# A fused attention/GLU kernel: the transposes of six token blocks in the first layer move from TensorE to the DMA queue

## Chip, cores and metric

The kernel runs on one core of one Trainium2 chip. The metric is device microseconds of one execution. The kernel before was timed three times: 381.76 us is the median, 380.99 us the lowest and 382.18 us the highest. Smaller is better. A separate execution was recorded by the hardware profiler; the durations below come from that one.

## The reference

Four layers act in turn on `x` of 2048 tokens by 448 features (bf16): attention, GLU, attention, GLU. Both attention layers use the same weights, and so do both GLU layers.

```python
x = x + A(layernorm(x), wqkv, wo)
x = x + B(layernorm(x), w_gate, w_up, w_down)
x = x + A(layernorm(x), wqkv, wo)
x = x + B(layernorm(x), w_gate, w_up, w_down)
# A: 16 heads of 28; token s attends to s, s-2, ..., s-14 (8 keys, those below 0 masked)
# B: ((x @ w_gate) * (x @ w_up)) @ w_down, inner width 1792
```

## The kernel before

**Tiling.** The tokens are 16 blocks of 128. Layer 0 takes them in five chunks: chunk 0 is blocks 0 and 1, chunk 1 blocks 2 to 5, chunk 2 blocks 6 to 9, chunk 3 blocks 10 to 13, chunk 4 blocks 14 and 15. A block is normalised on VectorE (statistics L593 and L595, the scaled block `xn_sb` L617, with the inverse deviation by ScalarE, L596 and L598). Its transpose goes to `xnTa`, where it feeds the matmuls that make K and Q (`qk_chunk`, line L356 through the helper `pair`) and V (`v_group`). `xn_sb` is a ring of five slots; a slot is free once the transpose that reads it is done.

**Two ways to transpose.** `ln_chunk` has both. If the name of layer and chunk stands in `PE_T`, TensorE transposes: for chunks 1 to 4, eight matmuls of 64x64 against an identity (L636), two running at once on the two halves of the array, into two PSUM banks, and one copy from PSUM to `xnTa` on ScalarE or VectorE (L646). Otherwise SP issues one DMA transpose of 128x512 from `xn_sb` to `xnTa` (L625). Before the change all five chunks of layer 0 are in `PE_T`; layer 2 uses the DMA for its 16 blocks, and the GLU layers use the DMA for two blocks at a time (L622). The DMA transposes of one chunk share one semaphore, and whoever needs one of the chunk's blocks waits for the chunk's full count.

**Attention.** For a group of up to 240 query tokens: `Qz` (L842, VectorE) spreads Q, scores on TensorE (L856), exponential on ScalarE (L865), mask on VectorE (L872), weighted sum on TensorE (L890), its way out of PSUM (L901, L905), normalisation (L919 to L921, L940), and the output projection (`y_blocks`). Group 0 is the first 128 tokens.

**GLU.** `b_chunk` makes gate and up (L356 with `WGU`), copies the gate out (L1014), multiplies (L1020) and projects down (L356 with `WD`).

**Order.** Nothing is scheduled at run time. Every piece of work is an "op" with a number given in the order in which it is created; `ORDER` lists for each engine the numbers in the order of issue, and `BANKS` the PSUM banks. An entry such as `372*2.4.5/363:3` puts three steps of op 363, cut into strips of 32 columns, between the matmuls of op 372 (the strips are line L359). Each engine takes its list strictly in turn: an op that waits holds up everything behind it. The two engine choices, "act" or "dve", are made by the list in which the number stands.

**The SP queue.** SP issues nearly all DMAs, in list order. The loads that matter here are numbers 72 to 83 (`WGU`, twelve pieces; a piece of the gate matrix may be issued once the one before it of the same matrix has landed, and the same for the up matrix), 84 to 87 (`wo_g`), 92 (`wo_h`), and 88 to 91 (`WD`: 88 after the last gate piece 82, 89 after the last up piece 83, 90 after 88, 91 after 89). The stores of the extra columns of `qk` to DRAM ("PW", L740) and the transposed loads of them (L751) stand in the same list.

**Numbers used below** (before / after; the change has six ops fewer, so later numbers shift by up to six):

| work | before | after |
|---|---|---|
| scaled blocks 10 to 15, VectorE | 177 180 183 186 195 198 | 177 179 181 183 191 193 |
| their transposes on TensorE | 178 181 184 187 196 199 | none |
| copy out of PSUM, or DMA transpose | 179 182 185 188 197 200 | 178 180 182 184 192 194 |
| `Qz` and scores of group 0 | 217, 218 | 211, 212 |
| first weighted sum 0, 1 | 223, 257 | 217, 251 |
| second half-V of query blocks 3 and 4 | 248 | 242 |
| first K/Q parts of chunk 3 | 456 458 460 | 450 452 454 |
| first K/Q part of chunk 4 | 534 | 528 |
| first use of `WD` | 317 | 311 |
| GLU transpose of blocks 0 and 1 | 295 | 289 |

Of the kernel before, what the change touches and what calls it, by code (L numbers as in the profile page):

```python
# [14 lines left out]
NBLK = S // 128  # L15
# [19 lines left out]
PE_T = ("00", "01", "02", "03", "04")  # L35
# [62 lines left out]
def grp_nc(g):  # L98
# [21 lines left out]
    ),  # L120
    "act": (
# [10 lines left out]
    ),  # L132
    "dve": (
# [19 lines left out]
    ),  # L153
# [7 lines left out]
    ),  # L161
}
BANKS = (
# [221 lines left out]
def build(nc, A_x, A_wqkv, A_wo, B_w_gate, B_w_up, B_w_down, out):  # L385
# [45 lines left out]
    sc = Sched()  # L431
# [731 lines left out]
```

## Time and profile before

| what | value |
|---|---|
| median of 3 runs | 381.76 us |
| the profiled execution, its own time | 381.87 us |
| its span, first to last instruction | 380.1 us |
| granted TensorE clock | 1.00 |
| DVE busy, ACT busy | 277.1 us, 194.6 us |
| DMA moved | 24.12 MB, mean 63 GB/s |

The span is what the trace shows; 1.77 us of the profiled execution's time lies around it. Busy time of TensorE is pipelined: the rows of a timeline overlap a little, so the distance from one row's start to the next one's is the time that the work takes on the engine's path. In the chain of waits (the work that ended last, followed back) the pieces do not overlap. PE stands for TensorE, DVE for VectorE, ACT for ScalarE, SPq for the DMA queue of SP.

### The profile page before, as it was taken

What the parts mean: (1) busy time and instruction counts of PE and PEld (TensorE: products, weight loads), DVE (VectorE), ACT (ScalarE), POOL (GpSimd) and SP (SyncE); (2) the same over time, 40 slices, a digit from 0 to 9 for tenths busy, and PEclk for the clock granted to TensorE, in tenths of its full rate; (3) what the DMA queues carried; (4) which work ended last, traced back from release to release, by engine and by line L of the source; (5) the groups of instructions that cost most, each with busy time, mean ns of one, the idle gap of its engine ahead of it and who ended that gap; (6) DMA issues with size and microseconds to landing.
All of it is one profiled execution on the core that took longest, in us unless ns stands there. A gap on an engine that the chain in (4) does not pass through costs nothing.

```text
span 380.1 us, 14239 instructions
## 1 busy us (share of the span) xinstructions
PE 374.5 (99%) x6388; PEld 210.7 (55%) x6388; DVE 277.1 (73%) x572; ACT 194.6 (51%) x327; POOL 5.1 (1%) x25
## 2 busy tenths in 40 slices
PE   8999999999999999999999999999999999999997
PEld 3654587544545445454866866554455454445664
DVE  7987999898795586778477989558888487274233
ACT  4999896567235565334365422546654634134110
POOL 5000000000000000000000000000000000000000
PEclk9999999999999999999999999999999999999999
DMA  8656646200522025112103125401123104104003
GB/s 259 169 149 156 148 124 104 56 18 23 97 40 45 2 50 84 33 32 56 28 2 62 28 43 111 63 10 32 25 50 71 43 3 83 26 2 98 2 2 109
DMA packets 58804, 24.12 MB, mean 63 GB/s; under 512 B 47928, under 2 KB 58616, under 8 KB 58744
## 3 DMA queue, kind: packets, MB, share of 16 engines
q1 hardware_dynamic: 58600, 23.16, 27.6%
q8 instruction: 50, 0.82, 0.9%
q14 instruction: 10, 0.08, 0.1%
q10 hardware_dynamic: 144, 0.06, 0.1%
HBM read 9.04 MB, written 3.50 MB: 33 GB/s over the span
## 4 chain that ended last, share of the span: by engine, by line
PE 95%; DVE 2%; ACT 2%; issue 0%; DVEq 0%
PE ps L356 84%; PE ps L359 4%; PE ps L856 2%; PE ps L890 2%; PE ps L510 2%; PE ps L1032 1%; ACT E_sb L865 1%; PE ps L636 0%; ACT qk L731 0%; DVE R_sb L919 0%; ACT xnTa L643 0%; DVE st L593 0%; DVE x_sb L981 0%; ACT R_sb L920 0%; ACT R_sb L921 0%
## 5 line engine op out<-in xcount | busy, mean ns | idle before, releaser
L356 PE MATMUL ps<-xnTb,WGU 64*128 64x512 bf16 (+1 forms) x1912 | 173.4, 332 | 0.1
L356 PEld LDWEIGHTS ps<-xnTb,WGU 64*128 64x128 bf16 x1912 | 93.4, 94 | 69.5 <-DVE x_sb L981 1.3
L1014 ACT ACTIVATE g_sb<-ps 128x512 bf16<-128x512 f32 x112 | 65.9, 596 | 100.6 <-PE ps L356 95.0
L1020 DVE TENSOR_TENSOR hT<-g_sb,ps 128x512 bf16<-128x512 bf16 x112 | 74.9, 682 | 55.4 <-ACT g_sb L1014 54.8
L356 PE MATMUL ps<-WD,hT 64*128 64x448 bf16 x786 | 80.6, 349 | 0.1
L356 PEld LDWEIGHTS ps<-WD,hT 64*128 64x128 bf16 x786 | 38.5, 94 | 33.0 <-issue 0.8
L356 PE MATMUL ps<-xnTa,WQK 64*128 64x512 bf16 (+1 forms) x494 | 52.3, 353 | 0.1
L981 DVE TENSOR_TENSOR x_sb<-x_sb,ps 128x448 bf16<-128x448 bf16 x62 | 36.3, 614 | 13.3 <-PE ps L356 13.2
L865 ACT ACTIVATE E_sb<-ps,shift_sb 128x1024 bf16<-128x1024 f32 (+1 forms) x36 | 37.5, 1071 | 14.1 <-PE ps L856 14.1
L593 DVE BATCH_NORM_STATS2 st<-x_sb 128x6 f32<-128x448 bf16 x64 | 38.1, 614 | 1.1 <-DMA x_sb<-in_A_x_dram 1.0
L356 PEld LDWEIGHTS ps<-xnTa,WQK 64*128 64x128 bf16 x494 | 22.8, 94 | 21.5 <-ACT E_sb L865 0.8
L731 ACT ACTIVATE qk<-ps 128x1024 bf16<-128x1024 f32 (+1 forms) x26 | 23.4, 909 | 13.9 <-PE ps L356 13.6
L617 DVE TENSOR_SCALAR xn_sb<-x_sb,mv,rstd 128x896 bf16<-128x896 bf16 (+1 forms) x64 | 28.2, 456 | 2.6 <-ACT rstd L598 2.5
L872 DVE TENSOR_TENSOR E_sb<-E_sb,MK 128x1024 bf16<-128x1024 bf16 (+1 forms) x36 | 23.4, 658 | 6.8 <-ACT E_sb L865 6.7
L356 PE MATMUL ps<-wo_g,oT 64*128 64x448 bf16 x147 | 25.5, 349 | 0.7 <-issue 0.7
L356 PE MATMUL ps<-WV,xnTa 64*128 64x336 bf16 (+3 forms) x240 | 23.1, 304 | 0.3 <-ACT xnTa L643 0.2
L920 ACT ACTIVATE R_sb<-R_sb 128x960 f32<-128x960 f32 (+1 forms) x18 | 17.2, 958 | 11.3 <-DVE R_sb L919 11.2
L919 DVE STREAM_SHUFFLE R_sb<-O_sb 128x960 f32<-128x960 f32 (+1 forms) x18 | 21.2, 1179 | 0.0
L940 DVE TENSOR_TENSOR oT<-O_sb,R_sb 128x960 bf16<-128x960 f32 (+1 forms) x16 | 17.5, 1094 | 3.9 <-ACT R_sb L921 3.9
L901 ACT ACTIVATE O_sb<-ps 128x512 f32<-128x512 f32 (+2 forms) x20 | 10.7, 558 | 16.5 <-PE ps L890 16.5
L596 ACT ACTIVATE lnv<-mv,eps_sb 128x2 f32<-128x2 f32 (+1 forms) x33 | 9.3, 290 | 16.5 <-DVE mv L595 16.3
L890 PEld LDWEIGHTS ps<-E_sb,v_sb 64*32 64x32 bf16 x1088 | 13.2, 90 | 8.0 <-issue 2.5
(68 smaller groups left out, 257.2 us busy)
## 6 DMA issues: line engine op xcount, KB each, us to landing
out_dram<-x_sb SPq DMA_DIRECT2D x15, 112.0 KB, 1.8
x_sb<-in_A_x_dram SPq DMA_DIRECT2D x3, 448.0 KB, 6.1
hT<-in_A_wqkv_dram SPq DMA_DIRECT2D x4, 224.0 KB, 4.6
WGU<-in_B_w_gate_dram SPq DMA_DIRECT2D x4, 224.0 KB, 4.1
WGU<-in_B_w_up_dram SPq DMA_DIRECT2D x4, 224.0 KB, 4.2
WD<-in_B_w_down_dram SPq DMA_DIRECT2D x2, 448.0 KB, 4.6
mv_rows<-oT SPq DMA_DIRECT2D x12, 64.0 KB, 1.8
oT<-mv_rows SPq DMA_DIRECT2D x48, 8.0 KB
```

The lines of the kernel that those rows point to most:

```text
L356: return lambda E: E.matmul(out(), lhs(), rhs(), start=start, stop=stop)
L593: sc.add("dve", one(lambda E, B=B: E.bn_stats(st6[:, B, :], x_sb[:, B, :]), ("bn", li, B)), 525.0, deps=[("x", li - 1, B)] + ([("xn", li - ...
L617: sc.add("dve", one(lambda E, B=B, dst=dst, src=src: E.tensor_scalar(dst, src, mv[:, B, 0:1], rstd[:, B:B + 1], ALU.subtract, ALU.mult), ( ...
L731: return E.activation(dst, src, ACT.Copy) if hasattr(E, "activation") else E.tensor_copy(dst, src)
L865: return E.activation(E_sb[:, slot, 2 * hp:2 * hp + 2, 0:w], ps[:, b0:b0 + 2, 0:w], ACT.Exp, bias=shift_sb[:, 0:1], scale=SCALE)
L872: return E.tensor_tensor(e, e, MK[:, kind, 0:nc].unsqueeze(1).unsqueeze(1).to_broadcast([128, 2, w // nc, nc]), ALU.min)
L890: ins.append((lambda E, b=b, c=c, o=o, vw=vw, eb=eb, eo=eo: E.matmul(ps[32 * b:32 * b + 32, bk[c], o:o + nc], vw, E_sb[64 * c:64 * c + 64, ...
L919: sc.add("dve", one(lambda E: E.stream_shuffle(R, Of, [DH] * 32), ("Rs", li, qb)), dve_est(w) + 20.0, deps=[("Oa", li, g)] + prev, prio=prio)
L940: return E.tensor_tensor(dst, O.rearrange("p d h n -> p h d n"), Rv.rearrange("p d h n -> p h d n"), ALU.mult)
L981: sc.add("dve", one(lambda E: E.tensor_tensor(x_sb[:, B, :], x_sb[:, B, :], ps[:, bk[w], 0:D], ALU.add), ("x", li, B)), dve_est(D), deps=[ ...
L1014: sc.add("act", one(lambda E, gs=gs, bk=bk: E.activation(g_sb[:, gs, :], ps[:, bk[0], :], ACT.Copy), ("G", li, j, f0)), act_est(512), deps ...
L1020: return E.tensor_tensor(hT[:, f0:f0 + nf, hs, 0:nt], v(g_sb[:, gs, :]), v(ps[:, bk[1], :]), ALU.mult)
```

## The change

Chunks 3 and 4 of layer 0 leave `PE_T`. Blocks 10 to 15 are then transposed by one DMA each (L625), six DMA transposes on SP instead of 48 matmuls on TensorE and six copies (four on VectorE, two on ScalarE). The wait list of `hT` no longer names TensorE transposes that do not exist. All lists in `ORDER` but POOL's, and all of `BANKS`, are new.

```diff
-PE_T = ("00", "01", "02", "03", "04")
+PE_T = ("00", "01", "02")
...
     "pe": (
-        "41 42 43 44 45 46 47 48 49 50 51 52 53 54 112 115 55 56 57 58 130 213 133 243 136 214 139 244 207 237 208 238 231 203 157 232 233 204 234 154 201 205 "
-        "202 206 235 160 163 236 218 327 181 328 196 252 325 223 326 187 323 184 178 324 247 257 458 248 199 459 456 460 534 461 535 457 270 329 265 530 266 "
...
+        "41 42 43 44 45 46 47 48 49 50 51 52 53 54 112 115 55 56 57 58 130 133 207 237 208 136 139 238 197 231 198 232 227 201 225 202 228 157 226 199 195 200 "
+        "196 163 229 160 154 230 212 321 246 322 319 217 320 317 241 318 251*3.5/242:2 450 452 454 453 455 451 528 323 529 264 324 259 524 260 333 525 334 456 "
...
     "dve": (
...
+        "15 17 103 39 104 16 107 108 119 117 111 120 118 114 123 125 129 126 124 132 59 131 141 135 138 61 65 137 142 62 143 40 187 144 173 171 174 172 156 185 "
+        "149 186 147 150 188 148 167 153 158 159 165 162 168 181 164 166 191 183 161 211 70 68 179 67 69 245 177 216 215 249 218 219 220 221 250 224 193 253 "
...
     "sp": (
-        "0 1 2 7 8 9 5 4 6 3 13 72 12 74 73 10 11 75 76 77 78 79 80 81 86 84 87 85 71 83 92 82 89 335 295 336 338 337 469 543 91 475 346 468 540 88 471 347 542 "
-        "90 470 398 481 480 476 401 101 102 496 99 95 98 97 94 500 96 497 100 499 498 541 93 519 548 521 523 520 522 553 547 614 617 687 685 568 689 691 569 "
...
+        "0 1 2 7 8 9 5 4 6 3 13 72 12 74 73 10 11 75 76 182 192 77 180 78 184 178 79 80 194 81 86 84 87 85 331 71 83 289 82 465 462 329 89 332 330 92 464 91 "
+        "341 463 88 340 469 90 392 475 470 395 536 98 474 97 101 102 490 534 535 100 96 93 537 493 494 492 94 491 542 99 95 513 541 514 515 516 517 608 547 546 "
...
-            war = hslot_users.get((hs, "prev"), WQKR + [("Tps", 0, B) for B in range(NBLK)] + [("vones",)])
+            war = hslot_users.get((hs, "prev"), WQKR + [("Tps", 0, B) for B in range(NBLK) if ("Tps", 0, B) in sc.ready] + [("vones",)])
```

Of the other ops each engine keeps the same ones, except that some copies out of PSUM change between ScalarE and VectorE: of the transposes that stay on TensorE, ScalarE copies blocks 7, 8 and 9 before and block 6 after, VectorE block 6 before and blocks 7, 8 and 9 after; the K/Q copy number 211 (205 after) and one of the eight copies of `WQK` (L518) go from VectorE to ScalarE. TensorE's list has 23 entries with strips before, with 70 strip steps, and 24 after, with 78.

106 rows, old and new, of tables (BANKS, ORDER) are left out of this document.

## The prediction

> **What bounds the kernel now.** I read the page's totals first, then its chain of waits.
>
> ```profile
> span 380.1 us, 14239 instructions
> PE 374.5 (99%) x6388; PEld 210.7 (55%) x6388; DVE 277.1 (73%) x572; ACT 194.6 (51%) x327; POOL 5.1 (1%) x25
> ...
> PE 95%; DVE 2%; ACT 2%; issue 0%; DVEq 0%
> ```
>
> TensorE is busy 99% of the span and holds 95% of the chain. What TensorE no longer does is saved, if nothing else makes it wait, and any new wait of TensorE is paid in full. I then looked at the stage where the six blocks are transposed: the chain from 20 to 32 us, and the group of these matmuls.
>
> ```profile
> 22.59 0.12 PE ps L636 x8
> ...
> 23.70 0.12 PE ps L636 x8
> ...
> 26.41 0.12 PE ps L636 x8
> ...
> 27.25 0.23 PE ps L636 x16
> ```
>
> ```profile
> L636 PE MATMUL ps<-hT,xn_sb 64*128 64x64 bf16 x112 | 3.7, 190 | 0.0
> ```
>
> The eight matmuls of a block hold the chain for 0.12 us. The group's 3.7 us for 112 is 0.26 us for eight, but there the head and tail of a run overlap with the next one. Next come the engines and the DMA in that stage (columns: length, PE, PEld, DVE, ACT and POOL busy, TensorE's granted clock, DMA share, GB/s):
>
> ```profile
> 20.00:30.00 10.00, 9.76 (x262) 5.07 (x256) 8.78 (x27) 9.69 (x17) 0.00 (x0) 1.00 0.56 140
> 30.00:40.00 10.00, 9.86 (x140) 4.98 (x137) 7.75 (x14) 8.51 (x11) 0.00 (x0) 1.00 0.75 181
> ```
>
> The clock is full, TensorE has under 0.3 us of idle in each ten, VectorE and ScalarE are close behind it, and the DMA engines have a quarter to a half left over.
>
> **The change, part by part.**
>
> *Removed on TensorE:* six blocks at 0.12 us are 0.72 us. Bounds: 0.72 by the chain and 6 x 0.26 = 1.6 by the group; I take 0.72, since the chain counts what TensorE's path really spends. The six copies out of PSUM (four on VectorE, two on ScalarE) cost nothing on the path while TensorE sets the pace; they give these two engines room.
>
> *Added strips:* the weighted sum of group 1 now carries two steps of the second half of V of query blocks 3 and 4.
>
> ```profile
> 28.84 0.68 PE L890 MATMUL ps<-E_sb,v_sb 64*32 64x64 bf16 x64
> 29.46 0.82 PE L356 MATMUL ps<-xnTa,WQK 64*128 64x512 bf16 x6
> 30.12 0.92 PE L356 MATMUL ps<-WV,xnTa 64*128 64x448 bf16 x8
> 30.87 0.28 PE L636 MATMUL ps<-hT,xn_sb 64*128 64x64 bf16 x8
> ```
>
> ```profile
> 72.10 0.25 PE L890 MATMUL ps<-E_sb,v_sb 64*32 64x64 bf16 x16
> ...
> 73.05 0.46 PE L356 MATMUL ps<-WV,xnTa 64*128 64x336 bf16 x4
> ```
>
> Alone such a sum takes 29.46 - 28.84 = 0.62 us. The one at 72.10 carries three steps and takes 0.95 us; a step of V is (30.87 - 30.12) / 4 = 0.19 us, so 0.95 - 0.57 = 0.38 us are its own. Two steps instead of three: I take 0.1 us saved, bounds 0 and 0.24.
>
> *Moved on VectorE: `Qz` of group 0 comes later.* Its list in the stretch before that (timeline of VectorE; the row at 18.72 is the scaled block 8, the one at 20.15 block 11, the two at 21.63 blocks 14 and 10):
>
> ```profile
> 10.47 0.64 DVE L518 COPY WQK<-hT 128x448 bf16<-128x448 bf16 x3
> ...
> 18.72 0.39 DVE L617 TENSOR_SCALAR xn_sb<-x_sb,mv,rstd 128x512 bf16<-128x512 bf16 x1
> ...
> 19.45 0.69 DVE L731 CAST qk<-ps 128x512 bf16<-128x512 f32 x1
> 20.15 0.41 DVE L617 TENSOR_SCALAR xn_sb<-x_sb,mv,rstd 128x512 bf16<-128x512 bf16 x1
> 20.48 0.61 DVE L842 TENSOR_SCALAR Qz<-qk,qmask 128x512 bf16<-128x512 bf16 x2
> ...
> 21.63 0.73 DVE L617 TENSOR_SCALAR xn_sb<-x_sb,mv,rstd 128x512 bf16<-128x512 bf16 x2
> ...
> 23.04 0.42 DVE L646 COPY xnTa<-ps 128x512 bf16<-128x512 bf16 x1
> ```
>
> ```profile
> 21.23 0.44 PE L856 MATMUL ps<-Qz,qk 64*64 64x144 bf16 x16
> ```
>
> Ahead of that `Qz` the new list has three scaled blocks of the last six (12, 14, 13) where the old one has one (11), three copies L646 (7, 9, 8) where the old one has one (6), no K/Q copy, and one weight copy less. A scaled block takes 20.48 - 20.15 = 0.33 us, a copy L646 about the same (0.42 with its overlap), the K/Q copy 0.70, the weight copy 0.2. So +0.66 + 0.66 - 0.70 - 0.2 = +0.42 us. The scores of group 0 start at 21.23, right behind `Qz`'s end at 21.09, and the ops ahead of them on TensorE are the same ones in both lists. So they come about 0.4 us later, and behind them everything on TensorE. Bounds: 0, if VectorE's waits before 18.7 us shrink, and 0.7; I take 0.4.
>
> *Moved on SP: six DMA transposes among the weight loads.* Their price is that of layer 2's (bottom two rows of this view: issue time of one on SP's queue, and time to landing):
>
> ```profile
> L625 SPq DMA_TRANSPOSE xnTa<-xn_sb x16: 1188/1200/2319, 109.3 to 243.6; - x16
> ...
> DMA to landing us min/median/max: 2.4/2.5/4.3
> ```
>
> So six of them add 7.2 us to SP's list. That queue before, where the rows at 17.99, 22.40, 30.06 and 36.31 are loads 76, 78, 81 and 82, those at 38.71 and 58.79 loads 89 and 90 of `WD`:
>
> ```profile
> 17.99 0.61 SPq L451 DMA_DIRECT2D WGU<-in_B_w_gate_dram  x1
> ...
> 22.40 0.59 SPq L451 DMA_DIRECT2D WGU<-in_B_w_gate_dram  x1
> ...
> 30.06 0.60 SPq L451 DMA_DIRECT2D WGU<-in_B_w_up_dram  x1
> ...
> 36.31 0.62 SPq L451 DMA_DIRECT2D WGU<-in_B_w_gate_dram  x1
> 38.71 0.40 SPq L451 DMA_DIRECT2D WD<-in_B_w_down_dram  x1
> ```
>
> I walk the new list from 18.6 us, the end of load 76. Block 12 is scaled at about 18.72 + 0.4 (blocks 9 and 12 instead of 8 alone) + 0.4 for its own run and overlap, say 19.6. Then: block 12 until 20.8, block 14 until 22.0, load 77 until 22.6, block 11 until 23.8, load 78 until 24.4, block 13 until 25.6, block 10 from 25.6 to 26.8. Block 10 is scaled right behind the `Qz` of group 1, at about 23.5, so SP's queue decides, not VectorE. It lands at 25.6 + 2.5 = 28.1, or at 29.9 with the longest landing of the row above; the four blocks of chunk 3 count together. Who waits: the first K/Q part of chunk 3. In the old order it starts at 29.46; without the five transposes ahead (0.6), with the V half ahead of it (0.75), the strips (-0.1) and the late scores (+0.4) it starts at about 29.9. The transposes land just in time or just late. The DMA engines were only half busy, so I take 0.2 us; bounds 0 and 2, the latter for a landing that two weight loads push back.
>
> ```profile
> DMA to landing us min/median/max: 3.4/4.2/6.3
> ```
>
> (That is the landing of the twelve `WGU` loads, whose range shows how far queueing goes: 2.1 us above the median.)
>
> The wait is felt at a second place: scaled block 15 takes the ring slot of block 10, so VectorE stops at it until chunk 3's four transposes have landed. In the new list it stands behind group 0's normalised output (L940):
>
> ```profile
> 31.41 0.68 DVE L940 TENSOR_TENSOR oT<-O_sb,R_sb 128x512 bf16<-128x512 f32 x1
> ```
>
> Fewer ops are ahead of that output now, so I put it at 29.5 to 31; behind block 15 are queued the sums and reciprocals of group 1. Block 15 goes out to SP at about 30.5 and lands at 33.0 to 34.8. Its reader, the first K/Q part of chunk 4, stands six K/Q parts behind that of chunk 3, three of 0.65 and three of 0.86, thus at 34.4. I take 0.1 us; bounds 0 and 1.
>
> *Later on SP: the weights.* Load 81 goes from 30.06 to about 31.7, which costs nothing. But now one `qk` store of chunk 2 stands ahead of loads 83 and 82, and the GLU transpose 289 ahead of load 82 and of all of `WD`. In the old list that transpose starts at:
>
> ```profile
> 44.54 1.64 SPq L622 DMA_TRANSPOSE xnTb<-xn_sb  x1
> ...
> 50.17 2.96 SPq L751 DMA_TRANSPOSE v_sb<-vt  x2
> ...
> 58.79 0.38 SPq L451 DMA_DIRECT2D WD<-in_B_w_down_dram  x1
> ```
>
> ```profile
> WD<-in_B_w_down_dram SPq DMA_DIRECT2D x2, 336.0 KB, 3.8
> ```
>
> ```profile
> 54.21 6.28 PE L356 MATMUL ps<-xnTb,WGU 64*128 64x256 bf16 x112
> ...
> 64.85 1.75 PE L356 MATMUL ps<-WD,hT 64*128 64x448 bf16 x14
> ```
>
> So load 82 is issued at about 46 instead of 36.31 and lands at 50.4 (median 4.2); the gate columns that it completes are first used in the third GLU step, which the row at 54.21 begins, some 3.5 us later. Load 89 comes at 48.5 instead of 38.71. Load 91 waits for its landing (some 53.1), then a transposed load of 1.5 us, a store, load 88 at 55.6, two more transposed loads, and load 90 when 88 has landed, at 59.4, about 0.6 later than in the row above. It lands at 63.2; `WD` is first read at about 64.5. These 1.3 us of slack hide it, so 0.
>
> *The rest.* All engines' lists differ to the end, with the same work in them. I price this at 0 with bounds of half a microsecond to either side, from the one stall of the middle that no op waits for:
>
> ```profile
> 74.64 0.66 issue
> ```
>
> It stands inside a run of one op's matmuls and may come back, go or double.
>
> **Sum**, against the profiled execution's 381.87 us: -0.72 - 0.1 + 0.4 + 0.2 + 0.1 = -0.12, thus 381.75, written 381.8. This is the median of the runs too (381.76), so nothing is to be corrected. A difference counts from 0.3%, some 1.15 us, which is about what a measurement of this kernel tells from no change.
>
> **Rivals.**
>
> *Faster, 380.5 us.* No new wait: the scores of group 0 are not late, the transposes land in time, and the 0.66 us stall goes: -0.72 - 0.66 = -1.38. For it: the DMA's free half, and the room that six copies leave. Against it: the late `Qz` is read straight from the list.
>
> *Slower, the landing, 383.7 us.* The six transposes and the loads 77, 78 and 79 share the DMA engines, so chunk 3 lands late. The place is the first K/Q part of chunk 3, the point from which it decides is a landing after 29.9 us, and its price is one for one. With the 2.1 us by which the longest `WGU` landing exceeds the median, chunk 3 lands 2 us late: 381.87 - 0.72 - 0.1 + 0.4 + 2.1 = 383.55, and 0.1 for block 15 makes 383.7. For it: the DMA share was 0.56 already, and VectorE stops at block 15 too. Against it: layer 2's transposes land in 2.5 us nearly always.
>
> *Slower, the weights, 383.2 us.* Load 90 is at the end of a chain of three landings. If each comes 0.9 us later than I took, `WD` lands at 65.9 and its first reader, at 64.5, waits 1.4 us: 381.8 + 1.4. For it: each landing has that spread. Against it: the queue is emptier after 45 us.
>
> *Slower, one by one, 397 us.* If a DMA transpose begins only when the one before it has landed, six at up to 4.3 us from 19.6 on end at 45.4, against 30 needed: some 15 us. Against it: the row at 50.17 shows two transposed loads issued back to back, where the second does not wait for the first one's landing. The Trainium skill (VectorE: DVE Perf Modes, "The three transpose paths" and its rules) advises TensorE for a 128x128 transpose wherever PSUM will do as destination, and gives 390 ns there against 1309 ns for the DMA. A block is four of these; by these figures an estimate is 1.6 us on TensorE against 5.2 us on the DMA, so the change would take 9 us from TensorE and put 31 us of transposing on the queue, which speaks against it if they run one by one. The trace disagrees on both: 0.12 us per block on TensorE's path, and 1.2 us of issue.
>
> **How the numbers follow.** Forecast 0.43 (its own range 380.8 to 382.9), faster 0.20, the landing 0.20, the weights 0.13, one by one 0.04. Thus faster 0.20, within 0.3% 0.43, slower 0.37. The range of 8 in 10 goes from 380.2, a little under the faster case, to 384.9, over the landing with the other order's half microsecond and some of the weights.
>
> **What would show it.** No L636 after 21 us, and L636's count 64. The scores of group 0 at 21.6 rather than 21.2. Six L625 rows between 19 and 32 us, landing in 2.5 to 4.3 us. TensorE's idle between 29 and 35 us: under 0.5 us speaks for the forecast, 2 us for the landing. Idle before the first `WD` matmul speaks for the weights. The forecast is wrong if TensorE waits over 1 us at one of these places, or if the time of one stage after 80 us differs by more than 1 us.

## The result, and the profile after

| | before | after |
|---|---|---|
| median of 18 runs each | 381.63 us (380.99 to 383.46) | 382.49 us (382.05 to 383.54) |
| ratio to before, 95% interval | | 1.0021 (1.0012 to 1.0029) |
| the profiled execution: its time, its span | 381.87 us, 380.1 us | 383.08 us, 381.0 us |

The change makes the kernel 0.2% slower, which is inside the 0.3% that I called no change and above the 381.8 us that I forecast. Of the 0.86 us between the medians about 0.3 lie outside the span, where neither the forecast nor the ledger below looks: a run's time less its span is 1.8 us in the kernel before (median of its runs in the experiments) and 2.05 to 2.15 us in all 18 runs of the changed one. Of the runs reported below one, at 388.59 us of the kernel with two loads moved, is left out as slow, since it lies over 1.5% above the fastest of its kernel. The totals of the page and the head of its chain of waits after:

```profile
span 381.0 us, 14257 instructions
...
PE 372.5 (98%) x6388; PEld 211.9 (56%) x6388; DVE 276.0 (72%) x568; ACT 194.8 (51%) x325; POOL 5.2 (1%) x25
...
PE 94%; DMA 2%; DVE 1%; ACT 1%; issue 1%; SPq 0%
```

TensorE works 2.0 us less than before (374.5), yet the span is 0.9 us longer: it waits 2.9 us more (the idle column of the ledger below). A new engine stands second in the chain, the DMA. The view of what TensorE waited for (us in total, times, longest) names the place; the second fence is the same view of the kernel before:

```profile
PE ps L356 <- DMA xnTa<-xn_sb: 2.2, 1, 2.2
...
PE ps L856 <- DVE WQK L526: 0.5, 1, 0.5
PE ps L856 <- ACT rstd L598: 0.5, 1, 0.5
```

```profile
...
PE ps L356 <- issue: 0.7, 1, 0.7
PE ps L856 <- DVE Qz L842: 0.2, 1, 0.2
PE ps L356 <- ACT xnTa L643: 0.2, 1, 0.2
```

One wait of 2.2 us for a transposed block is most of it. In TensorE's timeline after, it and the late scores of group 0 are these rows (in brackets the idle time before the row, and what ended it):

```profile
21.80 0.44 PE L856 MATMUL ps<-Qz,qk 64*64 64x144 bf16 x16 [0.48 <-DVE WQK L526]
22.42 0.82 PE L356 MATMUL ps<-xnTa,WQK 64*128 64x512 bf16 x6 [0.19 <-DVE WQK L526]
23.44 0.64 PE L856 MATMUL ps<-Qz,qk 64*64 64x128 bf16 x32 [0.20 <-DVE Qz L842]
...
32.47 2.77 PE L356 MATMUL ps<-xnTa,WQK 64*128 64x512 bf16 x24 [2.20 <-DMA xnTa<-xn_sb]
```

The row at 32.47 is the first K/Q part of chunk 3, ready to start at 30.27. What it waited for stands in SP's timeline, where the L625 rows are the six transposes (12 and 14, 11, 13 and 10, then 15) and the others loads 77 to 80:

```profile
19.61 2.62 SPq L625 DMA_TRANSPOSE xnTa<-xn_sb  x2
22.28 0.61 SPq L451 DMA_DIRECT2D WGU<-in_B_w_up_dram  x1
22.93 2.43 SPq L625 DMA_TRANSPOSE xnTa<-xn_sb  x1
25.41 0.60 SPq L451 DMA_DIRECT2D WGU<-in_B_w_gate_dram  x1
26.05 2.60 SPq L625 DMA_TRANSPOSE xnTa<-xn_sb  x2
28.70 0.60 SPq L451 DMA_DIRECT2D WGU<-in_B_w_up_dram  x1
31.30 0.59 SPq L451 DMA_DIRECT2D WGU<-in_B_w_gate_dram  x1
32.89 1.20 SPq L625 DMA_TRANSPOSE xnTa<-xn_sb  x1
```

The second of the two at 26.05 is block 10. The chain, and the landing times of all L625 after, show when it came:

```profile
27.38 5.04 DMA xnTa<-xn_sb
32.43 0.05 issue
32.47 6.13 PE ps L356 x62
```

```profile
DMA to landing us min/median/max: 2.4/2.5/6.2
```

It was issued at 27.38 and landed 5.0 us later. By the semaphores the six took 6.2, 5.4, 5.9, 5.8, 5.0 and 2.4 us; only block 15, with no other transpose in flight, took what most of layer 2's take.

**The ledger.** TensorE's last matmul ends 0.90 us later than before. I split that by its records: the idle time between matmuls, and for each matmul the distance from its start to the next one's, with idle taken out.

| us | before | after | difference |
|---|---|---|---|
| idle, 20 to 30 us (late `Qz`) | 0.24 | 0.86 | +0.62 |
| idle, the wait for chunk 3 | 0 | 2.20 | +2.20 |
| all other idle | 1.65 | 1.72 | +0.07 |
| transposes, L636 | 2.07 | 1.11 | -0.96 |
| warm-up matmuls ahead of the first load, L510 | 6.66 | 5.79 | -0.87 |
| all other matmuls | | | -0.16 |

The warm-up row belongs to that execution and not to the change: fourteen of these matmuls take 5.87 us in the one and 4.76 us in the other, as the clock record goes to 1.0 at 6.69 us in the one and at 4.46 us in the other. Their whole sum varied from 5.63 to 6.73 us over the profiled runs of this study. Of the 0.87 us, 0.43 come back at once as idle time ahead of 20 us (0.61 us against 0.18, inside "all other idle").

### The profile page after: what moved, and what is told of

Read it like the earlier page. It is cut to its first block, busy times and chain, and to the rows that moved or that the text cites. A ratio compares the mean times of both kernels' runs of the same rounds, so it can differ in the third digit from the quotient of the medians.

```text
span 381.0 us, 14257 instructions
## 1 busy us (share of the span) xinstructions
PE 372.5 (98%) x6388; PEld 211.9 (56%) x6388; DVE 276.0 (72%) x568; ACT 194.8 (51%) x325; POOL 5.2 (1%) x25
## 4 chain that ended last, share of the span: by engine, by line
PE 94%; DMA 2%; DVE 1%; ACT 1%; issue 1%; SPq 0%
PE ps L356 84%; PE ps L359 4%; PE ps L856 2%; PE ps L890 2%; PE ps L1032 1%; DMA xnTa<-xn_sb 1%; DMA x_sb<-in_A_x_dram 1%; DVE st L593 1%; PE ps L636 0%; ACT E_sb L865 0%; ACT qk L731 0%; SPq L451 0%; DVE O_sb L901 0%; DVE xn_sb L617 0%; ACT v_sb L823 0%
## 5 line engine op out<-in xcount | busy, mean ns | idle before, releaser
L356 PEld LDWEIGHTS ps<-xnTb,WGU 64*128 64x128 bf16 x1908 | 95.3, 94 | 68.1 <-issue 1.9
L356 PE MATMUL ps<-WD,hT 64*128 64x448 bf16 x782 | 79.8, 349 | 0.0
L356 PE MATMUL ps<-xnTa,WQK 64*128 64x512 bf16 (+1 forms) x490 | 51.4, 352 | 2.4 <-DMA xnTa<-xn_sb 2.2
L617 DVE TENSOR_SCALAR xn_sb<-x_sb,mv,rstd 128x512 bf16<-128x512 bf16 (+1 forms) x64 | 27.8, 451 | 6.4 <-ACT rstd L598 3.7
L731 ACT ACTIVATE qk<-ps 128x1024 bf16<-128x1024 f32 (+1 forms) x27 | 24.6, 925 | 10.5 <-PE ps L356 10.5
L920 ACT ACTIVATE R_sb<-R_sb 128x960 f32<-128x960 f32 (+1 forms) x18 | 17.3, 963 | 20.6 <-DVE R_sb L919 20.6
L921 ACT ACTIVATE R_sb<-R_sb 128x960 f32<-128x960 f32 (+1 forms) x18 | 17.2, 957 | 0.3
```

Source lines behind the costliest of these rows:

```text
L356: return lambda E: E.matmul(out(), lhs(), rhs(), start=start, stop=stop)
L617: sc.add("dve", one(lambda E, B=B, dst=dst, src=src: E.tensor_scalar(dst, src, mv[:, B, 0:1], rstd[:, B:B + 1], ALU.subtract, ALU.mult), ( ...
L731: return E.activation(dst, src, ACT.Copy) if hasattr(E, "activation") else E.tensor_copy(dst, src)
```

## The experiments

Numbers of ops are those of the kernel after, unless a diff says otherwise. "Landed" is read from the semaphores.

**Theory.** Chunk 3's transposes land late, because they share the DMA engines with weight loads; this wait is the loss. **Rival:** the new orders of the engines lose or gain by themselves, wherever the blocks are transposed.

### Two loads behind chunk 3's transposes

```diff
 "sp":
-... 76 182 192 77 180 78 184 178 79 80 194 81 ...
+... 76 182 192 180 184 178 77 78 79 80 194 81 ...
```

> The changed kernel with two weight loads (77 and 78) moved on SP's list from between the DMA transposes to behind block 10's. Theory (late landing): TensorE's 2.2 us wait for chunk 3's transposes comes from weight loads and instruction fetches in the same DMA queue; without the two loads block 10's transpose is issued about 24 us instead of 27.4 and lands by 28 (30 if an instruction fetch falls into it), so the wait falls to 0 to 1 us and the time by 1 to 2.2 us, to 380.3 to 381.5. Rival (one by one at about 2 us each, whatever else is queued): five transposes from 19.6 land at 30 or later, the wait shrinks by under 1 us and the time stays above 381.6. Rival (weights late instead): the first GLU matmul or the first WD matmul waits, the time stays above 382.

Measured: 384.93 us (382.61 to 387.38), ratio 1.0097 (1.0060 to 1.0135), and not the 380.3 to 381.5 expected. Chunk 3 landed at 29.7 and its wait went, but block 15, which stands behind loads 79 and 80 as before, went out at 32.4 and took 4.2 us instead of 2.4, so it landed at 36.6 (TensorE's timeline; line numbers one higher in this kernel):

```profile
36.73 2.61 PE L357 MATMUL ps<-xnTa,WQK 64*128 64x256 bf16 x20 [2.03 <-DMA xnTa<-xn_sb]
```

The columns of the next view are length, PE, PEld, DVE, ACT and POOL busy, TensorE's granted clock, DMA share and GB/s:

```profile
37.10:40.50 3.40, 3.40 (x52) 1.95 (x48) 0.69 (x1) 0.11 (x1) 0.00 (x0) 0.51 0.46 123
```

So the wait moved on by one chunk, and after it TensorE ran 3.4 us at half its clock, which costs about another 1.7 us. Block 10 itself, with no load among the five transposes any more, still took 4.4 us to land; the last section comes back to that.

### The four loads behind the first five transposes

```diff
 "sp":
-... 76 182 192 77 180 78 184 178 79 80 194 81 86 84 87 85 ...
+... 76 182 192 180 184 178 77 78 194 79 80 81 86 84 87 85 ...
```

The expectation says behind all six transposes, but the list puts loads 77 and 78 ahead of block 15's (194); only 79 and 80 stand behind all six.

> The changed kernel with the four loads 77, 78, 79 and 80 on SyncE behind all six transposes; nothing else moved. Theory (the late landings of chunks 3 and 4, set by weight loads between the transposes and by the fetches of instructions, cost the 2.2 us wait, and the orders behind them give about 1.8 us back): block 10's transpose lands by 29.7 us as in the run with two loads moved, block 15's is issued near 30.2 us and lands at 32.7 to 34.7 us, where its first matmul is due at about 34.7; both waits go (under 0.5 us in sum), no matmul of WQK, WGU or WD waits for a load by more than 0.5 us, and the time is 380.0 to 381.5 us. Rival 1 (the wait only moves to the weights, which start 5 us later): a matmul of WGU or WD, or the first v_sb product, waits 1 us or more, and the time is 382 us or more. Rival 2 (the new orders give nothing back by themselves, and what was regained was only slack made by the wait): the first chunk's wait goes but the lag behind the kernel before at the end stays at 0.9 us or more, and the time is 382 to 383 us.

Measured: 386.5 us, ratio 1.0116 (1.0097 to 1.0136). Both waits for `xnTa` are gone (block 10 landed at 30.3, block 15 at 33.3), and the score group behind chunk 3 comes at 36.57 instead of 38.53. That is the part of the theory that holds: it is the landing that cost those 2 us. The time expected was missed by 5 us, as the first rival says: the wait moved to a weight. For `wo_g`, last in the row of loads, is late now (TensorE's timeline, and the stretch after it, columns as above):

```profile
41.62 1.67 PE L356 MATMUL ps<-wo_g,oT 64*128 64x448 bf16 x8 [3.44 <-DMA wo_g<-in_A_wo_dram]
```

```profile
41.60:45.00 3.40, 3.38 (x22) 1.85 (x24) 0.00 (x0) 0.00 (x0) 0.00 (x0) 0.50 0.59 146
```

### `wo_g` ahead of the loads

The four loads of `wo_g` go behind block 10, and their rule of waiting for load 80 is dropped:

```diff
 "sp":
-... 76 182 192 180 184 178 77 78 194 79 80 81 86 84 87 85 ...
+... 76 182 192 180 184 178 86 84 87 85 194 77 78 79 80 81 ...
-        plain_dma("sp", dst, src, ("wo", j), "d_wo", deps=["c_wo", ("wg", 1, 1)], prio=-45)
+        plain_dma("sp", dst, src, ("wo", j), "d_wo", deps=["c_wo"], prio=-45)
```

> The changed kernel with SyncE's order behind load 76: the five transposes of blocks 12, 14, 11, 13 and 10, the four loads of wo_g (which lose their rule of waiting for load 80), block 15's transpose, and then the loads 77 to 81. Theory (the 2.2 us wait for block 10's landing is the whole of what was mis-sized, and the wait for wo_g in the run with four loads moved was only where that order sent it): no matmul waits over 0.5 us for xnTa, wo_g, WGU or WD; TensorE's idle time falls from 4.8 to about 2.6 us, the granted clock stays at 1.0, and the time is 2.0 to 2.5 us under the changed kernel's 382.5: 380.0 to 380.6 us, under the kernel before by 1 us or more. Rival (some load or transfer of the first 50 us is always late when transposes take the queue: the wait moves on to the weights WGU, due near 49 us): a wait of 1 us or more for WGU or for a DMA behind it, and 381.5 us or more.

Measured: 383.99 us (382.6 to 386.4), ratio 1.0070 (1.0043 to 1.0097). No wait between 24 and 42 us, as the theory says, but the time is 3.4 us over the most that it allowed; and then the rival. The first GLU matmul stands still:

```profile
51.20 3.23 PE L356 MATMUL ps<-xnTb,WGU 64*128 64x256 bf16 x56 [2.55 <-DVE oT L940]
```

The engine named there had long been done. The matmul starts 0.25 us after the transposed `xnTb` landed, which the DMA view of 43 to 45 us shows beside its neighbour, load 83 (KB each, median us from issue to landing):

```profile
WGU<-in_B_w_up_dram SPq DMA_DIRECT2D x1, 336.0 KB, 4.6
xnTb<-xn_sb SPq DMA_TRANSPOSE x1, 7.0
```

The median of `xnTb`'s landings in that run is 4.0 us. It looks like the loss of the change once more, 20 us later, on a transpose that the change never touched: behind a load, it lands 3 us late. The run that puts it ahead of that load, further down, tests this.

### `Qz` of group 0 ahead of block 13's scaling

The kernel of the last experiment, and on VectorE:

```diff
 "dve":
-... 181 164 166 191 183 161 211 70 68 179 ...
+... 181 164 166 191 161 211 70 68 179 183 ...
```

> As the run with wo_g ahead of the loads, and on VectorE the scaling of block 13 is moved from ahead of the first score group's Qz to behind the scaling of block 11. Theory (the 0.5 us wait of the first score group is that one scaling of 0.4 us, as forecast for the change): the wait of 0.48 us at 21.3 us falls to 0.1 us or less, the transposes land as before, and the time is 0.3 to 0.5 us under the other run of this pair. Rival (Qz waits for the product of Q and K and not for its place on VectorE, or the time is lost again at the next group): the same time within 0.2 us.

Measured: 384.36 us, ratio 1.0069 (1.0047 to 1.0092). Half a miss. The scores of group 0 come without a wait at 21.42, so they did wait for that scaling, but the K/Q part behind them now waits for the copies of the weights:

```profile
21.42 0.44 PE L856 MATMUL ps<-Qz,qk 64*64 64x144 bf16 x16
22.60 0.82 PE L356 MATMUL ps<-xnTa,WQK 64*128 64x512 bf16 x6 [0.74 <-DVE WQK L526]
```

Idle in 20 to 30 us is 0.91 us instead of 0.86. VectorE's whole stretch there is late, not one op of it. The time is that of the other run of this pair within the noise; its wait for `xnTb` is 3.15 us.

### The old orders with the new method

The lists of before; only the six matmul transposes and copies give way to DMA transposes on SP (numbers of before):

```diff
 "sp":
-... 76 77 78 79 80 81 ...
+... 76 182 197 77 179 78 188 185 79 80 200 81 ...
```

> The old lists with only the method changed: the six blocks' matmuls and copies taken out, six DMA transposes put among the weight loads of SP. Theory: the same late landing, TensorE waits 2 to 4 us for chunk 3 at about 29 us, and no better order behind it gives it back: 382.5 to 385 us. Rival (the new order, not the transposes, is what costs): the saved 0.72 us shows, 380.8 to 381.6.

Measured: 386.33 us, ratio 1.0114 (1.0093 to 1.0134). Chunk 3's wait is 2.84 us, ending at 32.61, and then:

```profile
31.60:38.40 6.80, 5.79 (x30) 2.12 (x32) 3.27 (x8) 1.79 (x3) 0.00 (x0) 0.50 0.74 175
```

TensorE works 5.79 us in this stretch, so about 2.9 us are the halved clock; but its three runs at full clock took 384.85 to 387.20 us too, so the new orders are better for this method than the old ones. By how much, this run doesn't tell.

### The new orders with the old method

All blocks on TensorE; before's lists up to about 31 us (TensorE's to its op 199, in a second version to 459), and the changed kernel's order behind. The second version takes out a wait of 0.7 us for a PSUM bank that the first one's joint had made.

> The old lists of all engines up to TensorE's transpose of block 15 (about 31 us), all transposes on TensorE, and behind that point the new lists' order for what is left. Theory (the new order is worth 1.8 us behind 55 us, and the transposes lose it at the front): no wait at chunk 3, faster than before by 1 to 2 us, 379.7 to 380.7. Rival (the gain behind 55 us is only slack that the late front gives back, which an engine in time cannot gain): 381.2 to 382.

> All sixteen blocks on TensorE with the orders of the kernel before up to some 31 us, and the changed kernel's orders behind, as in the first run of this kind, but with the cut on TensorE behind the K/Q part that waited there for its bank, so that the joint itself adds no wait for a bank. Theory (the orders behind 31 us are worth about 1 us whatever transposes the blocks): the 0.7 us wait at the joint goes, the lag at the end is -0.2 to -1.2 us against the kernel before, and the time is 380.3 to 381.4 us. Rival (the 1 us regained in the first splice was only the joint's own delay caught up again): the lag at the end stays at 0 to +0.4 us, and the time is 381.6 to 382.5 us.

Measured: 383.13 us, ratio 1.0037 (1.0024 to 1.0050), and 382.64 us, ratio 1.0019 (1.0009 to 1.0030). I had read from the first that the orders behind 31 us give about 1 us back, since its lag behind the kernel before shrank from 1.5 us (the score group at 42.8 us) to 0.4 us (the last matmul). The second refutes it: slower than before without the joint's wait. The lag of a score group isn't lost time where the two lists put different work ahead of it. Hence the ledger above, which counts idle and busy time.

### The last two blocks alone by DMA

The same two versions, with blocks 14 and 15 by DMA and the four of chunk 3 on TensorE (numbers of before):

```diff
 "sp":
-... 76 77 78 79 80 81 ...
+... 76 77 197 78 79 80 200 81 ...
```

> As e2_splice, but blocks 14 and 15 alone are transposed by DMA (behind loads 77 and 80); their readers start some 4 us later than chunk 3's. Theory: both land in time, 0.24 us of TensorE is saved, 0.1 to 0.4 us under e2_splice. Rival (a DMA transposition among weight loads lands 5 to 6 us late wherever it stands): block 15, issued at 30.7, lands at 36 and TensorE waits about 2 us, 1.5 to 2 us over e2_splice.

> As the second splice, with the two blocks of chunk 4 (14 and 15) transposed by DMA and the four of chunk 3 on TensorE. Theory (a transpose by DMA saves TensorE its 0.12 us a block and costs nothing where it lands ahead of its first use): blocks 14 and 15 land by 27 and 33.5 us, no matmul waits for xnTa, and the time is 0.2 to 0.9 us under that of the second splice, 379.9 to 381.2 us. Rival (what is saved on TensorE here is lost at the later waits for xnTb and v_sb, as in the first run of this kind): equal to the second splice within 0.3 us.

Measured: 382.36 us, ratio 1.0010 (0.9995 to 1.0024), and 382.04 us, ratio 1.0007 (0.9991 to 1.0022): 0.8 and 0.6 us under the splice of its kind. In both, blocks 14 and 15 land in time and no matmul waits for them: a DMA transpose that is in time costs TensorE nothing. How much it saves these runs don't settle, as 0.8 and 0.6 us are about twice what two blocks take on TensorE by the ledger (0.96 us for six), and the intervals of the second pair overlap. The second kernel was expected at 379.9 to 381.2 us and is not that fast.

### The transpose of `xnTb` ahead of its load, in two kernels

```diff
 "sp":
-... 331 71 83 289 82 ...
+... 331 71 289 83 82 ...
```

In the kernel with `wo_g` ahead of the loads:

> As the run with wo_g ahead of the loads, with the first transpose of xnTb moved ahead of load 83 on SyncE. Theory (a transpose by DMA is late only where weight loads are issued between its neighbours or just ahead of it; with each of them ahead of the loads no wait is left): the 2.55 us wait for xnTb falls to 0.5 us or less, no other wait over 0.5 us comes, the granted clock stays at 1.0, and the time is 380.0 to 381.2 us, under the kernel before by 0.5 us or more. Rival (the transpose of xnTb was late by the fetches of instructions, which no order on SyncE moves): the wait stays at 1.5 us or more, and the time within 383 to 385 us.

In the last splice:

> As the third splice (blocks 14 and 15 alone by DMA, without the joint's wait), with the first transpose of xnTb moved ahead of load 83 on SyncE. Theory (as for the other run of this pair): the wait of 0.43 us for xnTb goes or stays, with nothing else changed, and the time is 0 to 0.5 us under that splice's 382.0 us: 381.3 to 382.0 us. Rival (the later load 83 makes the GLU wait for WGU): 382.5 us or more.

Measured: 381.40 us, ratio 0.9998 (0.9980 to 1.0016), and 382.80 us, ratio 1.0018 (0.9998 to 1.0038). In the first the wait for `xnTb` is gone (landed after 4.4 us, at 48.2, read at 50.1). In the second it is not: 0.89 us where the splice without the move had 0.43, and the time lies above the 381.3 to 382.0 us expected. Six of the first kernel's twelve runs lay from 380.12 to 380.73 us, six from 382.07 to 383.15. The profiled one is of the upper six and shows two waits:

```profile
62.56 0.25 PE L890 MATMUL ps<-E_sb,v_sb 64*32 64x64 bf16 x16 [0.66 <-DMA v_sb<-vt]
67.30 1.50 PE L356 MATMUL ps<-WD,hT 64*128 64x448 bf16 x14 [1.32 <-DVE mv L595]
```

The second row waits for load 90, the last of `WD`: issued at 62.26 when load 88 had landed, it landed at 67.10. The other kernel waits 1.56 us at the same place. This is the rival that I had called the weights. That it parts the two groups of runs is argued here, and tested next.

### The last load of `WD` earlier

On top of the first of these two, load 90 goes right behind load 88, and waits for load 82 instead of 88:

```diff
 "sp":
-... 91 341 463 88 340 469 90 ...
+... 91 341 463 340 88 90 469 ...
-    ... else [("wd", n - 2)], prio=-44)
+    ... else [("wg", 1, 2)] if n == 2 else [("wd", n - 2)], prio=-44)
```

> As the run with the first transpose of xnTb ahead of load 83, and the fourth load of WD (90) issued right behind the third (88), both behind the first two transposes of v_sb but one, and load 90 waiting for load 82 in place of load 88. Theory (half of the runs before lay near 380.3 us and half near 382.5 us, and the profiled one, of the upper half, waited 1.3 us for the fourth load of WD and 0.7 us for v_sb): load 90 lands by 65.5 us, the wait of 1.3 us ahead of the product of WD goes, the upper group goes with it, and the median is 380.0 to 381.0 us, at least 0.6 us under the kernel before. Rival (another transfer of the crowded stage becomes the late one, as in each run of this kind so far): the median stays at 381.2 us or more, with a wait of 0.7 us or more at a transfer between 50 and 75 us.

Measured: 380.57 us (379.88 to 380.95), against 381.39 us for the kernel before on the same chip; ratio 0.9972 (0.9963 to 0.9982). It beats both kernels. Totals, chain, and all that TensorE waits for behind its first instruction:

```profile
span 378.5 us, 14257 instructions
...
PE 372.9 (99%) x6388; PEld 211.7 (56%) x6388; DVE 276.1 (73%) x568; ACT 194.8 (51%) x325; POOL 5.2 (1%) x25
...
PE 98%; ACT 1%; issue 0%; DVE 0%
```

```profile
PE ps L856 <- ACT rstd L598: 0.5, 1, 0.5
PE ps L856 <- DVE WQK L526: 0.5, 1, 0.5
PE ps L856 <- DVE Qz L842: 0.2, 1, 0.2
PE ps L356 <- DVE WQK L526: 0.2, 1, 0.2
```

Load 90 landed at 63.5, the upper group of runs is gone, and no wait for a DMA is left. This execution's warm-up matmuls take 6.66 us as in the one of before, and its span is 1.5 us shorter: 1.0 us for the transposes, most of the rest the other matmuls, which are packed a little closer. The medians differ by 0.8 us only. The profiled execution of the kernel before (381.87 us) lies 0.5 us above its median here, and this kernel, like the changed one, has 0.3 us more outside its span.

## Why the prediction was right about the time and wrong about its cause

- *Removed on TensorE*: 0.72 us forecast, 0.96 measured, inside its bounds. The chain's 0.12 us for a block counts from the end of the matmul before, and leaves out what the run's head and tail add to its neighbours.
- *Strips*: 0.1 us saved forecast, 0.2 measured, inside its bounds. The sum of group 1 with its two steps takes 29.73 - 28.93 = 0.80 us; less two steps of 0.19 us, 0.42 are its own, against 0.62 alone:

```profile
28.93 0.28 PE L890 MATMUL ps<-E_sb,v_sb 64*32 64x64 bf16 x24
...
29.73 0.55 PE L356 MATMUL ps<-WV,xnTa 64*128 64x448 bf16 x4
```

- *`Qz` of group 0 late*: 0.4 us forecast; the scores came at 21.80 (0.57 late), and the idle of that stage grew by 0.62 us. The size is a little small, and its make-up is not the one I counted: VectorE stood still for 0.53 us ahead of a copy, until TensorE had made the transpose that it copies.

```profile
19.61 0.42 DVE L646 COPY xnTa<-ps 128x512 bf16<-128x512 bf16 x1 [0.53 <-PE ps L636]
```

- *The landing*: **the step that failed.** Block 12 went out at 19.61, as I had it (19.6), but by luck: VectorE had scaled it by 19.1 us, and it stood behind load 76, which went out at 18.96 instead of the 17.99 that I started from. Then I took 1.2 us for each issue and 2.5 us for a landing, and a wait of 0.2 us, because "the DMA engines were only half busy". The third transpose's issue took 2.43 us and the loads between kept their places, so block 10 went out at 27.38 instead of 25.6, and it landed in 5.0 us. The term of 0.2 us measured 2.20, past the 1 us that I had named as the sign of a wrong forecast. The price came from layer 2's transposes, which I read as 2.5 us "nearly always": by the semaphores eleven of the sixteen took 2.4 to 2.5 us, and the other five 3.5 to 4.3. In the five kernels that have no load among the first five transposes and show the landing, block 10 took 4.1 to 4.4 us. So the loads between are worth some 0.6 to 1.0 us of its 5.0, and the time of their issue; the rest of what is over 2.5 us stays without them (last section). The rival "the landing" had the place, the condition and the wait right (2.1 us), its time of 383.7 us 1.2 us too long, and the loads as the cause only in part.
- *VectorE at block 15's ring slot*: it stopped as foreseen, until chunk 3 had landed:

```profile
32.45 0.41 DVE L617 TENSOR_SCALAR xn_sb<-x_sb,mv,rstd 128x512 bf16<-128x512 bf16 x1 [2.47 <-DMA xnTa<-xn_sb]
```

Block 15 then landed at 35.3, nearly 1 us past the 34.4 at which I had its reader, which cost nothing as the reader was late with it.
- *The weights*: no wait before the first `WD` matmul in the changed kernel, as forecast (it starts at 67.57, right behind a V part), but with luck: load 90 landed at 65.67, 2.5 us later than I had it, and its reader was 3 us late. In two later kernels it came, with 1.3 and 1.6 us.
- *The rest*: the 0.66 us stall did not come back, and waits of 0.5 and 0.2 us near 45 and 52 us took its place; the 0 taken for it held.
- *One by one* is refuted: two transposes issued 1.35 us apart landed 0.6 us apart (25.83 and 26.40).

In the profiled execution the errors do not cancel: 2.0 us too little for the landing and 0.22 for `Qz` stand against 0.24 too little for the transposes, 0.1 for the strips, 0.1 taken for block 15 that cost nothing, and 0.87 us of an early start; with the 0.3 us outside the span its time lies 1.3 us over the forecast. That the median lies within 0.7 us is luck, as the mechanism was wrong. Not settled: the profiled execution lies 0.6 us above its own median, so in most of the runs the wait, or something else, is shorter than in the trace read here. One thing that varies is load 76: ahead of it SP's list is the same in all kernels, and it goes out at 17.99 to 19.20 us in the fourteen traces.

## What to carry to other kernels

Price a DMA that is moved between others by landings among such neighbours, and where only a quiet stage shows its kind, look at all of its landings and not at their median: here they fall into two groups, and the upper one (median 4.0 us) was the better guess. When a transfer is put ahead of others on one in-order queue, list the deadline of every transfer behind it: here one wait of 2.2 us went from chunk 3 to chunk 4, to `wo_g`, to the GLU's transpose and to `WD`, and only the order that met all five deadlines was faster than the kernel before. To compare two orders, count idle and busy time, not the lag of landmarks.

## What the runs showed of the hardware

**A wait of 2 us can halve the clock, by where it falls.** The clock records change on a grid of 3.413 us: TensorE ran at 0.5 for 3.41 us after waits of 2.03 and 3.15 us, for 6.83 us after 2.84 and 3.44 us, and not at all after waits of 2.20 us (the changed kernel) and 2.55 us. What parts them is the share of one step of the grid that was idle: 1.80 us or more in the halved cases, 1.5 and 1.6 us in the two others, whose waits lay across a step's edge (the edges there taken from the last change of the record). The second half-speed step came where the wait's remainder of 0.8 or 1.0 us lay in it. In two kernels the halved clock goes with the spread of the runs: with two loads moved, the fastest run (382.61 us) had a mean clock of 1.0 and the others (384.84 us and more) 0.996; with `wo_g` ahead, the three of 1.0 took 382.6 to 383.1 us and the three of 0.996 384.9 to 386.4. All 18 runs of the changed kernel had 1.0, and spread over 1.5 us. The Trainium skill (TensorE: Matmul & The Clock Gate, "What's actually happening") gives a free-running window of 3413 ns and an idle window as what slows the clock. The grid agrees; but here about half a window of idle was enough.

**A transpose beside an instruction fetch mostly lands late.** The fetches of instructions stand on queues of their own in the page (kind: packets, MB, share of 16 engines):

```profile
q1 hardware_dynamic: 61864, 23.94, 31.3%
q8 instruction: 50, 0.82, 0.9%
```

In the changed kernel the DMA records show two fetches of 16 KB in the stage of the six transposes, at 23.06 and 28.86 us, of 1.22 and 1.34 us each. From 22.6 and from 29.5 us on, some of the transposes' packets take up to 2.5 and 1.5 us (nine in ten take under 0.04), and their flow resumes at 25.0 and 31.0 us. Layer 2, where no weight load is issued, gives a count. The fourteen traces have 224 landings of such transposes there: 153 took 2.40 to 2.65 us and 71 took 2.90 to 4.65. A fetch of 16 KB was under way within 2.4 us of the issue for 68 of the 71 late ones and for 21 of the 153 others. The median of the 68 is 4.0 us, so an estimate of what goes with a fetch is 1.6 us. Block 10's 4.1 to 4.4 us without a load among the transposes fit this, as a fetch was under way in all five traces. That the fetch is the cause is not shown, as no run took the fetches away.

**Packets move in the order of issue.** The transposes' packets have 256 bytes, 512 for a block. In the changed kernel 1024 of them move from 21.9 to 25.6 us, 512 from 27.0 to 28.1, 1024 from 28.9 to 31.5 and 512 from 34.1 to 34.8, and between these mostly packets of 1792 bytes, the size of a row of a load (224 KB in 128 rows). These are two blocks, one, two and one, as SP issued them among the loads.
